# Interleaved rows, wider value tiles and earlier weights in a fused sliding-window attention and gated-unit kernel

## The chip, the cores and the metric

The kernel runs on one core of one Trainium2 chip. The metric is the device time of one execution in microseconds (us), the median of several. A core has a matrix engine (TensorE, PE in the profile; its weight loads are PEld), VectorE (DVE), ScalarE (ACT), GpSimd (POOL), SyncE (SP), and 16 DMA engines that move data between device memory (HBM) and the on-chip memory. Transfers are issued from the queues of SP, ACT and POOL.

## The reference

Eight batches, eight heads, 576 positions, head size 64, all float32. Heads 0 to 3 see the 32 positions up to their own ("plain"), heads 4 to 7 see every fourth of the last 128 ("dilated"). The attention output, 512 wide, goes into a gated unit: a causal depthwise convolution of five taps gives the gate, `w_val` the value, `w_out` the output.

```python
scores = scale * np.matmul(q, k.transpose(0, 1, 3, 2))
mask_plain = (rel >= 0) & (rel < window)                                   # window 32
mask_dil = (rel >= 0) & (rel < window * dilation) & (rel % dilation == 0)  # dilation 4
attn = softmax(where(mask, scores, -1e9)); x = (attn @ v) with heads side by side
gate_pre += conv_w[k][None, None, :] * xp[:, k:k + S, :]                   # for k in range(5)
gate = 1.0 / (1.0 + np.exp(-gate_pre)); val = x @ w_val
return (gate * val @ w_out)
```

## The kernel before

**Work.** The unit of attention is a pair of heads; there are 32 pairs, four to a batch, dilated and plain in turn (`order`, line 216). For each pair `attend` (L532) makes scores (`scores`, L460) into two PSUM banks, exponentials on ACT (L463), a multiplication by a 0/1 mask on DVE or POOL (L468), the product with v (L477 plain, L487 and L491 dilated), the division by the row sum on DVE (L496, L497), a transpose (L514, L518) and a copy into `xT` (L388 on ACT, L390 on DVE). When a batch has its four pairs, `gated` (L638) makes for each of four chunks the convolution (L591), a tanh (L648), the value product (L601) and gate times value (L652), and then the output product (L609), its copy to `osb` (L614, L616) and the store to HBM (L666). Each batch has 64 rows that don't fill a tile; `y_rem` (L659) collects them over four batches, and L673 stores them, twice in a kernel, two stores each.

**Loads of q and k.** Two batches, four heads of one kind, are a group, cut into three tiles of 128 partitions (`rows`, L311; `load_rows`, L328, issued at L331). Tile u = 0 is the first batch's first 128 partition rows, u = 2 the second batch's last 128, and the middle tile, u = 1, takes 64 rows of each batch. A partition row is 3072 bytes: one transfer of 384 KB for a dilated tile; for a plain middle tile two of 192 KB. There are 4 groups x 2 kinds = 8 middle tiles for q and 8 for k. A dilated tile is transposed as it stands (`transpose_in`, L377 to L384, by a product with the identity `ident`); a plain one is first cast on POOL into `qc` or `kc` (L414). The transposed tile goes to `qT` or `kT` on ACT or DVE.

**Loads of v.** A dilated pair has two tiles, `va` (partition rows 0 to 95) and `vz` (rows 64 to 143, so 80 rows), loaded at L362 and cast by POOL at L560 into `vda` and `vdb`. A plain pair has one tile `vp`, loaded by one transfer at L368 and two at L371, in pieces of 256 bytes.

**Weights.** `load_w` (L700) loads `w_val` and `w_out` by POOL's queue, three transfers each (L704, L705), casting on the way. `ldwv` is due after the load of the plain middle tile of q in group 0, `ldwo` after v of pair 4. Copies on ACT and DVE put `w_val` in order (L715), then two transfers of SP (L718, `swap_out`) make the second copy of `w_out`.

**Order.** `Plan.run` (L52) simulates the kernel at build time with the costs given to `add`, and emits every task in the order so found; the engines run their queues in that order. For a transfer it takes bytes and a rate (`lag`). In the built program the transfers of SP and ACT share eight semaphores in turn, and the issue of a transfer waits until the one before it on its semaphore has landed. So a store in ACT's queue can wait for a load that SP issued up to eight transfers ahead, and what is behind the store on ACT waits too.

Of the kernel before, what the change touches and what calls it, by code (L numbers as in the profile page):

```python
# [33 lines left out]
class Plan:  # L34
# [7 lines left out]
    SLACK = 0.1  # L42

# [8 lines left out]
    def run(self):  # L52
# [13 lines left out]
        while todo:  # L66
# [45 lines left out]
            if t.lag:  # L112
                free[e] = est + c
                nbytes, rate = t.lag
                if e == "SP":
# [22 lines left out]
def kernel(  # L138
# [48 lines left out]
    vas = bufs(NVD, [96, 2, R * D], FP32, "va")  # L187
    vzs = bufs(NVD, [80, 2, R * D], FP32, "vz")
    vd0 = bufs(NVD, [96, 2, R, DA], BF16, "vda")
    vd1 = bufs(NVD, [80, 2, R, DA], BF16, "vdb")  # L190
# [71 lines left out]
    def c_spread_p():  # L262
# [3 lines left out]
                              mask_p[:, None, 96:192].to_broadcast([128, 6, 96]))  # L266

# [33 lines left out]
    K_sp = add("sp", -5, {"DVE": 0.9}, lambda t: c_spread_p(), [K_mp])  # L301
    K_id2 = add("id2", 0.5, {"DVE": 0.4}, lambda t: c_ident2(), [K_ident])
# [8 lines left out]
    def rows(kind, u):  # L311
# [21 lines left out]
    def unit(n, kind):  # L333
        for u in range(3):
            first = 8 * n + (0, 2, 4)[u] + (kind == "p")
            for w, (nm, ring, src) in enumerate((("q", qs, q), ("k", ks, k))):
# [7 lines left out]
                    "ld" + nm, first + 0.1 * w, 393.0 / len(pieces), 330.0,  # L344
# [6 lines left out]
    def load_v(i):  # L351
# [25 lines left out]
    def transpose_in(t, kind, src):  # L377
        ps = bank(t, BF16)
        for f in range(6):
# [4 lines left out]
            nc.tensor.transpose(out=ps[:, f * 128:f * 128 + 128], in_=lhs, identity=ident)  # L384
# [17 lines left out]
    def prepare(n, kind, u):  # L402

        prio = 8 * n + (0, 2, 4)[u] + (kind == "p")
        for nm in "qk":
# [4 lines left out]
            if kind == "p":  # L410
# [9 lines left out]
            tr = U["tr"] = add("tr", prio - 0.05, {"PE": 0.34}, lambda t, src=src: transpose_in(t, kind, src),  # L420
                               got + [K_ident], banks=1, mode="full")
# [11 lines left out]
    def scores(t, i, hf, qT, kT):  # L433
# [3 lines left out]
        for x in range(2):  # L437
            rb = slice(x * D, x * D + D)
            if is_dil(i):
# [5 lines left out]
                for n in range(2):  # L445
                    g0 = ((b % 2) * 4 + 2 * (g - 2) + n) * 48
                    o = hf * 3 * G + 3 * g0 + 64
# [332 lines left out]
```

## Time and profile before

| what | value |
|---|---|
| median of 3 runs (lowest to highest) | 361.05 us (357.87 to 362.71) |
| profiled execution, its time | 360.51 us |
| profiled execution, its span | 358.80 us |
| PE busy, PEld busy | 208.7 us, 140.9 us |
| DVE, ACT, POOL busy | 129.2 us, 110.1 us, 57.5 us |
| moved by DMA | 42.33 MB, mean 118 GB/s |
| mean granted clock of TensorE | 0.793 |
| last PE instruction ends | 348.3 us |

The profile is of one execution. "PE busy" counts matmuls; PEld overlaps it. The page cuts the span into 40 slices of 8.97 us and gives each engine's busy share in tenths. "DMA" is the mean busy share of the 16 DMA engines. The chain is followed back from the last instruction, at each step to what released it. A line such as "ACT qTd L388 <- DMA k" names the idle engine, the instruction that then ran, and what released it; where one wait is for several things, the one that came last.

### The profile page before, as it was taken

To read this page: it belongs to the slowest core of one execution; us is meant where nothing else is said; L and a number is where in the kernel's file an instruction comes from. 1 tells how busy PE (TensorE), PEld (TensorE's weight loads), DVE (VectorE), ACT (ScalarE), POOL (GpSimd) and SP (SyncE) were. 2 spreads that over 40 slices of the span, in tenths; PEclk is the share of its full clock that TensorE was granted. 3 is DMA by queue.
4 is the path that set the end of the run, shared out by engine and by line. 5 is a ranking of instruction groups with operands and counts; after the bars stand their busy time and mean duration, and the time that the engine had idled before them with its cause. 6 is when DMAs were issued, how large, how long until landed. Compare 5 with 4: busy or idle time off the path is not lost.

```text
span 358.8 us, 5844 instructions
## 1 busy us (share of the span) xinstructions
PE 208.7 (58%) x2452; PEld 140.9 (39%) x2452; DVE 129.2 (36%) x221; ACT 110.1 (31%) x174; POOL 57.5 (16%) x98
## 2 busy tenths in 40 slices
PE   3317055755028766678616575756672787666970
PEld 2214044535024534545414453434432565444530
DVE  5313116643012435344600534441340366345240
ACT  3123035141032333430214244534023445413420
POOL 6203035060100041003500041030100031020000
PEclk9999999978556868655955989886576599766997
DMA  7225399921169146321277029222139421100331
GB/s 238 67 84 96 91 271 244 206 87 54 50 216 237 47 136 201 97 87 50 74 220 239 2 50 321 60 82 83 50 90 294 134 46 60 60 0 2 119 119 58
DMA packets 47490, 42.33 MB, mean 118 GB/s; under 512 B 26851, under 2 KB 39656, under 8 KB 47464
## 3 DMA queue, kind: packets, MB, share of 16 engines
q1 hardware_dynamic: 41424, 31.46, 31.9%
q10 hardware_dynamic: 4920, 9.45, 7.1%
q0 software_dynamic: 1120, 1.05, 2.0%
q8 instruction: 19, 0.31, 0.4%
q14 instruction: 7, 0.06, 0.1%
HBM read 33.04 MB, written 9.44 MB: 118 GB/s over the span
## 4 chain that ended last, share of the span: by engine, by line
PE 41%; DMA 14%; DVE 14%; ACT 11%; SPq 11%; issue 4%; POOL 1%; ACTq 1%; DVEq 0%; POOLq 0%
DMA k<-in_k_dram 11%; PE ps L601 11%; PE ps L609 10%; PE ps L591 7%; SPq L331 7%; ACT et L463 6%; DVE xn L497 5%; DVE y L652 5%; PE ps L384 5%; ACT gate L648 3%; SPq L371 3%; PE ps L460 3%; DVE rec L496 2%; PE ps L477 2%; DMA va<-in_v_dram 2%
## 5 line engine op out<-in xcount | busy, mean ns | idle before, releaser
L601 PE MATMUL ps<-xT,w_val 128*128 128x288 bf16 x256 | 48.9, 352 | 11.6 <-ACT et L463 4.8
L463 ACT ACTIVATE et<-ps 128x576 bf16<-128x576 f32 x64 | 39.9, 650 | 43.9 <-PE ps L460 14.4
L591 PE MATMUL ps<-xT,conv_d 64*64 64x288 bf16 x640 | 37.2, 377 | 20.3 <-ACT osb L614 12.6
L609 PE MATMUL ps<-w_out,y 128*128 128x512 bf16 x128 | 40.3, 455 | 7.2 <-DVE xn L497 4.1
L601 PEld LDWEIGHTS <-w_val 128*128 128x128 bf16 x256 | 29.1, 118 | 25.9 <-issue 11.8
L614 ACT ACTIVATE osb<-ps 128x512 f32<-128x512 f32 x33 | 19.5, 597 | 53.2 <-PE ps L609 27.9
L652 DVE SCALAR_TENSOR_TENSOR y<-gate,ps 128x576 bf16<-128x576 bf16 x32 | 23.6, 751 | 31.9 <-PE ps L601 14.3
L591 PEld LDWEIGHTS <-conv_d 64*64 64x64 bf16 x640 | 23.4, 136 | 27.3 <-issue 22.6
L496 DVE RECIPROCAL rec<-ps 96x8 f32<-96x8 f32 (+1 forms) x48 | 10.1, 210 | 62.6 <-ACT et L463 23.7
L648 ACT ACTIVATE gate<-ps 128x576 bf16<-128x576 f32 x32 | 20.3, 652 | 34.0 <-PE ps L591 9.6
L390 DVE COPY xT<-ps 128x576 bf16<-128x576 bf16 x15 | 11.4, 757 | 51.9 <-ACT gate L648 18.5
L460 PE MATMUL ps<-qTd,kTd 64*128 64x96 bf16 (+1 forms) x256 | 10.8, 223 | 29.4 <-ACT gate L648 22.3
L497 DVE TENSOR_TENSOR xn<-ps,rec 96x512 bf16<-96x512 f32 (+1 forms) x32 | 26.2, 820 | 1.1
L659 POOL COPY y_rem<-y 128x256 bf16<-128x256 bf16 x8 | 3.2, 399 | 139.0 <-DVE y L652 139.0
L388 ACT COPY xT<-ps 128x576 bf16<-128x576 bf16 x17 | 10.9, 639 | 41.2 <-DVE y L652 16.7
L609 PEld LDWEIGHTS <-y 128*128 128x128 bf16 x128 | 13.4, 112 | 24.0 <-issue 17.1
L460 PEld LDWEIGHTS <-kTd 64*128 64x128 bf16 x256 | 8.3, 111 | 34.1 <-issue 31.2
L468 DVE TENSOR_TENSOR et<-et,mask_d 128x1152 bf16<-128x1152 bf16 x15 | 12.4, 827 | 25.4 <-ACT et L463 25.4
L560 POOL CAST vda<-va 96x512 bf16<-96x512 f32 x16 | 10.6, 664 | 65.1 <-DMA va<-in_v_dram 32.1
L468 DVE TENSOR_TENSOR et<-et,mask_p 128x1152 bf16<-128x1152 bf16 x14 | 13.1, 938 | 13.9 <-ACT et L463 13.9
L460 PE MATMUL ps<-qTp,kTp 64*128 64x96 bf16 x192 | 9.3, 226 | 9.7 <-DVE y L652 3.9
L384 PE MATMUL ps<-ident,qc 128*128 128x128 bf16 x72 | 7.8, 261 | 11.4 <-POOL qc L414 5.0
(73 smaller groups left out, 256.4 us busy)
## 6 DMA issues: line engine op xcount, KB each, us to landing
out_dram<-osb ACTq DMA_DIRECT2D x16, 512.0 KB
q<-in_q_dram SPq DMA_DIRECT2D x20, 384.0 KB
k<-in_k_dram SPq DMA_DIRECT2D x20, 384.0 KB
vp<-in_v_dram SPq DMA_DIRECT2D x32, 160.0 KB
va<-in_v_dram SPq DMA_DIRECT2D x16, 192.0 KB
vz<-in_v_dram SPq DMA_DIRECT2D x16, 160.0 KB
q<-in_q_dram SPq DMA_DIRECT2D x8, 192.0 KB
k<-in_k_dram SPq DMA_DIRECT2D x8, 192.0 KB
```

The source lines that it names most:

```text
L331: nc.sync.dma_start(out=dst[:, o:o + w], in_=bass.AP(tensor=src.tensor, offset=base + off, ap=ap))
L384: nc.tensor.transpose(out=ps[:, f * 128:f * 128 + 128], in_=lhs, identity=ident)
L460: nc.tensor.matmul(out=o, lhsT=l, rhs=r, start=True, stop=True)
L463: nc.scalar.activation(out=et[:, hf * 576:hf * 576 + 576].rearrange("p (b c) -> p b c", b=2), in_=ps[:, :, 0:HALF], func=AF.Exp, scale=scale)
L468: eng.tensor_tensor(out=et[:, 0:ET], in0=et[:, 0:ET], in1=(mask_d if is_dil(i) else mask_p)[:, 0:ET], op=ALU.mult)
L497: nc.vector.tensor_tensor(out=xo, in0=av[:, :, :, 0:D], in1=rec[:, :, 0:n, None].to_broadcast([96, 2, n, D]), op=ALU.mult)
L591: nc.tensor.matmul(out=ps[ob:ob + D, half, 0:HALF], lhsT=conv_d[x * D:x * D + D, c, kk, :], rhs=xT[x * D:x * D + D, c, s:s + HALF], start= ...
L601: nc.tensor.matmul(out=ps[:, half, 0:HALF], lhsT=w_val[half][:, mc, c * 128:(c + 1) * 128], rhs=xT[:, mc, s:s + HALF], start=(mc == 0), st ...
L609: nc.tensor.matmul(out=ps[:, :], lhsT=cols(c), rhs=w_out[half][:, c, :], start=(c == 0), stop=(c == NCH - 1))
L614: nc.scalar.activation(out=osb, in_=ps, func=AF.Copy, scale=0.5)
L648: th = add("tanh", base + 1.0 + 0.5 * c, {"ACT": 0.66}, lambda t, cv=cv, gt=gt: nc.scalar.activation(out=gt, in_=banks(cv, 2)[:, :, 0:HALF ...
L652: y = add("y", base + 1.2 + 0.5 * c, {"DVE": 0.76}, lambda t, c=c, vl=vl, gt=gt: nc.vector.scalar_tensor_tensor(out=y_all[:, c, b % NY, :] ...
```

## The change

The core of the diff (each hunk is whole where the text speaks of it):

```diff
+    TRANSFER = 1.1
...
                 nbytes, rate = t.lag
+                rate /= self.TRANSFER
...
-    vas = bufs(NVD, [96, 2, R * D], FP32, "va")
-    vzs = bufs(NVD, [80, 2, R * D], FP32, "vz")
-    vd0 = bufs(NVD, [96, 2, R, DA], BF16, "vda")
-    vd1 = bufs(NVD, [80, 2, R, DA], BF16, "vdb")
+    vas = bufs(NVD, [128, 2, R * D], FP32, "va")
+    vzs = bufs(NVD, [128, 2, R * D], FP32, "vz")
+    vd0 = bufs(NVD, [128, 2, R, DA], BF16, "vda")
+    vd1 = bufs(NVD, [128, 2, R, DA], BF16, "vdb")
...
-    y_rem = consts.tile([128, NCH, 2, B, 32], BF16, name="y_rem")
+    y_rem = consts.tile([128, NCH, 2, 2, 32, 4], BF16, name="y_rem")
+    ident_x = consts.tile([128, 128], BF16, name="ident_x")
...
-        band(mask_d[:, 192:240].rearrange("p (m t) -> p m t", m=3), 32, [[1, 3], [3, 16]], 1)
+        band(mask_d[:, 192:240].rearrange("p (m t) -> p m t", m=3), 96 - (T - 128), [[1, 3], [3, 16]], 1)
...
+    def c_identx():
+        nc.vector.tensor_copy(ident_x.rearrange("p (b r) -> p b r", b=2), ident.rearrange("p (r b) -> p b r", b=2))
...
-            part, off = [[step, 2], [r * D, 64]], 128 * r * D
+            part, off = [[r * D, 64], [step, 2]], 128 * r * D
...
-                    "ld" + nm, first + 0.1 * w, 393.0 / len(pieces), 330.0,
+                    "ld" + nm, first + 0.1 * w, 393.0 / len(pieces), 390.0 if kind == "d" else 330.0,
...
-            for x, (dst, r0, n) in enumerate(((vas[j % NVD], 0, 96), (vzs[j % NVD], 64, 80))):
-                P["lv"].append(ld("ldv", i + 0.2 + 0.1 * x, n * 2.05, 240.0,
+            for x, (dst, r0, n) in enumerate(((vas[j % NVD], 0, 128), (vzs[j % NVD], T - 128, 128))):
+                P["lv"].append(ld("ldv", i + 0.2 + 0.1 * x, n * 2.05, 380.0,
...
-            nc.tensor.transpose(out=ps[:, f * 128:f * 128 + 128], in_=lhs, identity=ident)
+            nc.tensor.transpose(out=ps[:, f * 128:f * 128 + 128], in_=lhs, identity=ident_x if u == 1 else ident)
...
-                    nc.tensor.matmul(out=ps[:, x, c * DA:(c + 1) * DA], lhsT=et[0:96, o:o + 128],
+                    nc.tensor.matmul(out=ps[:, x, c * DA:(c + 1) * DA], lhsT=et[:, o:o + 128],
...
-                    nc.tensor.matmul(out=ps[:, x, c * DA:(c + 1) * DA], lhsT=et[0:80, o:o + 128],
+                    nc.tensor.matmul(out=ps[:, x, c * DA:(c + 1) * DA], lhsT=et[:, o:o + 128],
...
-                    out=out[b - 3:b + 1, half * HALF + 256:half * HALF + HALF, :], in_=osb[:, half, :]), 262.0)
+                    out=out[b - 3:b + 1, half * HALF + 256:half * HALF + HALF, :].rearrange("b n d -> n b d"),
+                    in_=osb[:, half, :]), 262.0)
...
     wv = add("ldwv", 1.0, {"POOL": 2.6}, lambda t: load_w(t, w_out[1], moe_w_val),
-             [UNIT[0, "p", 1, "q"]["ld"][0]], lag=(1049.0, 330.0))
+             [PAIR[1]["lv"][0]], lag=(1049.0, 330.0))
...
     wo = add("ldwo", 5.0, {"POOL": 2.6}, lambda t: load_w(t, w_out[0], moe_w_out),
-             [PAIR[4]["lv"][0]], lag=(1049.0, 330.0))
+             [PAIR[3]["lv"][0]], lag=(1049.0, 330.0))
```

In words. The middle tile's partitions take rows of the two batches in turn (row 0 of the first, row 0 of the second, row 1 of the first), where before the first 64 were one batch and the last 64 the other. The transpose of a middle tile uses `ident_x`, the identity with its columns permuted, which puts the rows back in the old order; all transposes now wait for its making. `va` and `vz` have 128 partitions (rows 0 to 127, and 16 to 143), and the dilated products with v contract over 128 partitions. The mask of the second part is moved to fit. `y_rem` holds the four batches of a row side by side, and its stores walk row by row with the batch inside. `ldwv` is due after the first piece of v of pair 1, `ldwo` after v of pair 3. The planner's rates are changed (also that of stores, from 340 to 400), and all are divided by 1.1, so that it orders some tasks differently. In the built program PE, DVE, ACT and POOL have nearly the same lists as before: POOL's mask multiplications go from 3 to 2 (DVE's from 29 to 30), ACT's copies of `w_val` from 2 to 4 (DVE's from 6 to 4). POOL issues `ldwv` ahead of the two casts of pair 2's v where it was behind them, and `ldwo` ahead of the first cast of pair 4's v. In SP's queue the two `swap_out` transfers come seven loads earlier, ahead of the first tile of group 1.

More of the change, by code (lines that the diff above doesn't have):

```diff
@@ L301 @@
     K_sp = add("sp", -5, {"DVE": 0.9}, lambda t: c_spread_p(), [K_mp])
+    K_idx = add("idx", 0.4, {"DVE": 0.2}, lambda t: c_identx(), [K_ident])
     K_id2 = add("id2", 0.5, {"DVE": 0.4}, lambda t: c_ident2(), [K_ident])
@@ L374, in load_v, with transpose_in @@
                                 ap=[[D, 128], [96 * D, NB - 1], [1, D]])), dep))
-    def transpose_in(t, kind, src):
+    def transpose_in(t, kind, src, u):
         ps = bank(t, BF16)
@@ L419, in prepare @@
                 src = c
-            tr = U["tr"] = add("tr", prio - 0.05, {"PE": 0.34}, lambda t, src=src: transpose_in(t, kind, src),
-                               got + [K_ident], banks=1, mode="full")
+            tr = U["tr"] = add("tr", prio - 0.05, {"PE": 0.34}, lambda t, src=src: transpose_in(t, kind, src, u),
+                               got + [K_idx], banks=1, mode="full")
             if kind == "d":
@@ L446, in scores @@
                     g0 = ((b % 2) * 4 + 2 * (g - 2) + n) * 48
-                    o = hf * 3 * G + 3 * g0 + 64
+                    o = hf * 3 * G + 3 * g0 + T - 128
                     todo[x].append((ps[:, x, 192 + n * 48:240 + n * 48], kT[rb, o:o + 128],
@@ L558, in attend @@
             c0, c1 = vd0[j % NVD], vd1[j % NVD]
-            for x, (s, d, n) in enumerate(((vas[j % NVD], c0, 96), (vzs[j % NVD], c1, 80))):
+            for x, (s, d) in enumerate(((vas[j % NVD], c0), (vzs[j % NVD], c1))):
                 P[f"cv{x}"] = add("cv", i - 0.2, {"POOL": 0.62}, lambda t, s=s, d=d: nc.gpsimd.tensor_copy(
@@ L634, in out_tiles @@
             ots.append(ot)
-        out_st.append([add("st", prio + 0.5, {"ACT": 0.40}, lambda t, e=e: e(osb), oes, lag=(nb, 340.0)) for e, nb in store])
+        out_st.append([add("st", prio + 0.5, {"ACT": 0.40}, lambda t, e=e: e(osb), oes, lag=(nb, 400.0)) for e, nb in store])
         return ots
@@ L659, in gated @@
         YB[b] = add("yrem", base + 3.0, {"POOL": 0.35}, lambda t: nc.gpsimd.tensor_copy(
-            y_rem[:, :, :, b, :], yv[:, :, :, 256:HALF]), ys)
+            y_rem[:, :, :, b // 4, :, b % 4], yv[:, :, :, 256:HALF]), ys)
         YO[b] = [YB[b]]
@@ L670, in gated @@
             out_tiles(base + 5.2, [
-                (half, lambda c, half=half: y_rem[:, c, half, b - 3:b + 1, :].rearrange("p b n -> p (b n)"), deps)
+                (half, lambda c, half=half: y_rem[:, c, half, b // 4, :, :].rearrange("p n b -> p (n b)"), deps)
                 for half in range(2)],
                 [(lambda osb, half=half: nc.scalar.dma_start(
-                    out=out[b - 3:b + 1, half * HALF + 256:half * HALF + HALF, :], in_=osb[:, half, :]), 262.0)
+                    out=out[b - 3:b + 1, half * HALF + 256:half * HALF + HALF, :].rearrange("b n d -> n b d"),
+                    in_=osb[:, half, :]), 262.0)
                  for half in range(2)])
```

## Prediction

> **What bounds the kernel now.** I read the page's 40 slices first, then stretches, then the queues of ACT and SP around the longest idle time of PE.
>
> ```profile
> PE   3317055755028766678616575756672787666970
> PEclk9999999978556868655955989886576599766997
> DMA  7225399921169146321277029222139421100331
> GB/s 238 67 84 96 91 271 244 206 87 54 50 216 237 47 136 201 97 87 50 74 220 239 2 50 321 60 82 83 50 90 294 134 46 60 60 0 2 119 119 58
> PE 41%; DMA 14%; DVE 14%; ACT 11%; SPq 11%; issue 4%; POOL 1%; ACTq 1%; DVEq 0%; POOLq 0%
> ```
>
> No engine is full. PE has holes near 15, 24, 42, 95, 183 and 272 us, and each follows slices at 50 to 100 GB/s. A quarter of the chain is DMA and SP's queue. In the stretches below the columns are length, busy time of PE, PEld, DVE, ACT and POOL (instructions), PE's granted clock, DMA share, GB/s. The first two show a plateau, the next two the DMA at work on other loads.
>
> ```profile
> 20.00:26.00 6.00, 0.00 (x0) 0.00 (x0) 0.76 (x1) 0.48 (x1) 0.00 (x0) 1.00 0.13 51
> 84.00:99.00 15.00, 2.06 (x51) 1.70 (x49) 2.03 (x3) 0.00 (x0) 2.00 (x3) 0.72 0.13 50
> 2.00:10.00 8.00, 2.98 (x33) 2.28 (x34) 4.38 (x9) 3.45 (x5) 5.08 (x20) 1.00 0.91 273
> 48.00:60.00 12.00, 7.05 (x105) 5.37 (x103) 6.22 (x6) 6.74 (x10) 6.91 (x9) 1.00 1.19 243
> ```
>
> 0.13 is 2 of 16: two DMA engines work, 14 stand, while middle tiles load (outermost count 2 in HBM). Tiles with 128 outermost run at 273 GB/s. The queues show how PE gets stuck:
>
> ```profile
> 86.61 7.28 SPq L331 DMA_DIRECT2D k<-in_k_dram  x2
> ```
> ```profile
> 102.06 0.45 ACTq L666 DMA_DIRECT2D out_dram<-osb  x1
> 102.61 0.80 ACT L388 COPY qTd<-ps 128x768 bf16<-128x768 bf16 x1 [19.36 <-DMA k<-in_k_dram]
> ```
>
> SP issues the plain middle tile of k at 86.6; the last byte comes at 102. A store in ACT's queue waits for it by the shared semaphore, and with it everything on ACT behind the store: 19.36 us idle. PE then has nothing to do. The holes:
>
> ```profile
> 12.30:17.10 4.80, 0.02 (x1) 0.02 (x2) 0.69 (x1) 0.80 (x1) 0.00 (x0) 1.00 0.26 77
> 19.20:26.40 7.20, 0.05 (x1) 0.00 (x0) 0.76 (x1) 1.19 (x2) 0.00 (x0) 1.00 0.16 55
> 35.60:47.30 11.70, 0.82 (x6) 0.56 (x7) 1.45 (x3) 0.65 (x1) 1.65 (x2) 1.00 0.45 122
> 87.10:104.60 17.50, 0.04 (x2) 0.04 (x3) 0.06 (x1) 1.90 (x3) 2.00 (x3) 0.60 0.28 92
> 177.20:189.10 11.90, 1.41 (x20) 1.04 (x20) 0.43 (x1) 1.74 (x3) 0.00 (x0) 0.59 0.72 213
> 268.50:276.90 8.40, 1.42 (x20) 0.98 (x20) 0.00 (x0) 1.75 (x4) 0.83 (x1) 0.69 0.91 270
> ```
>
> Length less PE's busy time: 4.8 + 7.2 + 10.9 = 22.9 us at the start, 17.5 at 95, and 10.5 + 7.0 in the last two, 57.9 us in all.
>
> **The change part by part**, against the profiled execution's 360.5 us (span 358.8 and 1.7 around it; the median of the runs is 0.5 above).
>
> *Middle tiles interleaved.* The outermost count in HBM becomes 64. Counts of 128, 4 and 2 in this trace went at 16, 4 and 2 engines (273, 102 and 50 GB/s; the 102 is below), so I take 16. The same bytes in rows of the same length: a 384 KB tile takes 393/50 = 7.9 us now and 393/273 = 1.4 us then. The holes go: -57.9. What is late next?
> - Start. The last load that PE waits for is the second piece of the plain middle tile of k, SP's 17th transfer. Up to it there are 8 tiles of q and k (3.15 MB), two dilated v (1.05 MB, new size), one plain v (0.39 MB) and the first weights (1.05 MB): 5.6 MB at 273 GB/s is 20.6 us, and with 3 us for the first transfer (issued at 0.8, used at 4.0) 23.6 us. PE came there at 39.8, less the 15.4 us of holes before: 24.4. So it just fits. Bounds 0 and 5 (the rate 225 instead of 273, below the 243 of the row with 256-byte pieces); I take 2, near the fit.
> - Pair 8. PE came to it at 104.6, less 22.9 and 17.5: 64 us. It needs all of group 0 (4.72 MB), v of pairs 0 to 8 (4.2), weights (2.1), the swap (0.5), its own first tile (0.8): 12.3 MB, at 243 GB/s 51 us, and 3. It fits by 10. SP is also blocked while the swap waits for the copies of `w_val`, which now stands ahead of the seven loads that pair 8 and its followers need; in the old trace the swap was issued at 62.4 after a wait of 1.7. Bounds 0 and 8, I take 3.
> - Stores in ACT's queue still wait for the load on their semaphore. Eight transfers ahead at 1.0 to 1.4 us each, most landed already: 0 to 6 over the three places, I take 2.
>
> *v over 128 partitions.* It adds (32 + 48) x 2 KB x 16 = 2.6 MB, some 10 us of DMA at 273 GB/s over the kernel, hidden: the share of the DMA is 0.43 at most in the stretches between the holes. What precedes the 17th transfer is counted above. POOL's casts (614 ns for 96 as for 80 partitions), the products and the weight loads have the same free sizes: 0, and not more than 32 casts x 0.05 = 1.6 us on POOL, which has 57.5 busy of 358.8.
>
> *Identity.* One copy on DVE of 128 x 128; its nearest row, a 128 x 512 copy to `w_val`, took 0.28 us. It is covered by the first load, used at 4.0. Cost 0, and 0.3 if that cover were gone.
>
> *Weights earlier.* Three issues on POOL (0.69 + 0.69 + 0.73 = 2.1 us) come ahead of the two casts of pair 2's v. Those end 2.1 us later; who waits is the product with v of pair 2, behind scores, two exponentials and a mask. 0 to 2.1; I take 1. The transfers' bytes are in the sums above. The software queue took 2.0% of 16 engines, 7.2 us for both weights. The Trainium skill ("DMA: Bandwidth & Descriptors", section "Issuing engines are not separate DMA queues") speaks against this edit: transfers of all queues share the same 16 engines and interleave, so weights put ahead of the start's loads delay them; by that rule alone 3.6 us, half of the 7.2, would be added, and the sum would be 307.
>
> *Remainder stores.* The last two stores are the end of the chain:
>
> ```profile
> GB/s 0 0 0 0 0 0 0 370 353 0 0 331 370 45 0 0 0 0 0 0 0 0 141 384 198 379 345 34 11 56 76 102 102 102 102 102 37 0 0 11
> 348.39 1.21 ACTq L673 DMA_DIRECT2D out_dram<-osb  x2
> ```
>
> The slices are 0.725 us from 330 on. Two stores of 262 KB take 5.1 us at 102 GB/s; at the 370 of the stores before them 1.4. The row count 32 comes outermost instead of the batch count 4: -3.7, bounds -4.5 (latency shared) and 0.
>
> *Clock.* Half clock follows some holes:
>
> ```profile
> 104.60:114.60 10.00, 8.64 (x69) 4.80 (x69) 2.67 (x4) 2.78 (x5) 0.00 (x0) 0.50 0.92 251
> 148.70:169.00 20.30, 16.52 (x162) 11.54 (x162) 8.86 (x14) 6.25 (x10) 2.36 (x1) 0.50 0.23 73
> 333.00:345.00 12.00, 10.86 (x111) 6.67 (x109) 4.78 (x7) 3.82 (x7) 0.40 (x1) 1.00 0.24 89
> ```
>
> With the hole at 95 gone, the 10 us behind it may run at full clock and save up to half of 8.6. But 148.7 to 169 shows half clock with PE 81% busy and no hole before it. Bounds -15 (half of the PE time in two such stretches and the parts after the later holes) and +10 (one more stretch like the middle one); I take -4, the stretch right behind the hole. The Trainium skill ("TensorE: Matmul & The Clock Gate", section "HAM oscillation") holds that gaps over about 3.4 us throttle the array to half; the first row agrees, the second does not. By the rule alone no hole would mean full clock: PE's 41% of the chain, 147 us at 0.793, would be 117, and the sum 277.
>
> Sum: 360.5 - 57.9 + 2 + 3 + 2 + 1 - 3.7 - 4 = 302.9, so **303 us**. Cross-check: pair 8 to 16 took 87.9 us and 16 to 24 took 84.5 (by the exponentials at 105.0, 192.9, 277.4); less their holes, 77.4 each; from 277.4 to the end 81.4, less 3.7. With pair 8 at 64 that gives 64 + 3 x 77.5 + 1.7 = 298.
>
> **Rivals.**
> - *B, half of the holes come back.* The loads are spread, but the order of SP's and ACT's queues, and the 256-byte pieces of v, keep PE waiting. For: in 48 to 60 the DMA share is above 1 and PE only 59% busy. Against: that stretch makes up for two plateaus. Half of 57.9 is 29, in place of my allowances of 7: 303 + 22 = 325.
> - *C, the clock gains more.* All stretches as 333 to 345. Down to the bound: 303 - 11 = 292, and with nothing late, 284.
> - *D, the loads stay on two engines*, because the split goes by something other than the outermost count. Then only the stores gain: 360.5 - 3.7 = 357. Against: the counts 128, 4 and 2 above.
> - *E, slower.* One mechanism: PE's clock. Where PE never rests, half clock is granted throughout, as in 148.7 to 169. 147 us of PE on the chain would be 147 x 0.793/0.5 = 233: 303 + 86 = 389. It decides from a mean clock of 0.57 down (147 x (0.793/0.57 - 1) = 57). Against: 333 to 345, busiest of all, at 1.00.
>
> **How the numbers follow.** The forecast 0.71 (its own range 288 to 318), B 0.15, C 0.08, D 0.03, E 0.03. Low end: 360.5 - 57.9 - 3.7 - 15 = 284. High end: no clock gain and all upper bounds, 298.9 + 5 + 8 + 6 + 2 = 320, and on past B's 325 to 328. That leaves out half of B, some of C, D and E, under 2 in 10. Faster by over 2% (about what a measurement of this kernel can tell from no change): 0.71 + 0.15 + 0.08 = 0.94; within 2%: D, 0.03; slower: E, 0.03.
>
> **What would show it.** Right: no stretch at 0.13 DMA share and 50 GB/s; ACT's wait of 19.36 us gone, PE's first hole over 3 us near 12 us short or absent; pair 8's exponentials at 62 to 70 us; the last two stores in under 2 us. Wrong: middle tiles still at 50 GB/s (D); holes as long behind ACT's stores or SP's swap (B); a mean clock under 0.6 (E).

## The result and the profile after

The changed kernel takes 276.23 us (median, 275.91 to 276.66) beside 361.88 us for the kernel before on the same chip: 0.766 of its time, 95% interval [0.760, 0.773]. The forecast was 303 (284 to 328): the direction was right, and the gain of 85.6 us was under-estimated by 27. The profiled execution took 275.91 us, its span 274.2, and the mean granted clock is 0.842 where it was 0.793. The ratios here and below leave out runs over 1.5% above the fastest of their kernel, while the medians hold every run.

The slices of the changed kernel, 6.86 us each, and the shares of its chain:

```profile
PE   3766598688764677875766557778666686968772
PEclk9997779999977757997779975589999956865999
DMA  7999999991895505880039791095401410000306
GB/s 244 335 280 312 254 299 323 329 334 31 267 305 156 207 2 122 252 278 2 0 66 325 195 306 70 20 327 162 148 2 48 122 43 2 0 2 13 143 2 229
PE 52%; DVE 19%; ACT 13%; DMA 7%; issue 4%; SPq 3%; ACTq 0%; DVEq 0%
```

The runs of slices at 50 to 100 GB/s are gone, and so are the empty digits of PE between its second slice and its last. DMA and SP's queue go from 25% of the chain to 10%, PE from 41% to 52%. In the stretches, each from the first exponential of pair 8, 16 and 24 to the next, the columns are length, busy time of PE, PEld, DVE, ACT and POOL (instructions), granted clock, DMA share and GB/s. Before:

```profile
0.00:105.00 105.00, 42.61 (x563) 31.50 (x564) 33.97 (x66) 27.21 (x42) 26.64 (x54) 0.90 0.55 138
105.00:192.90 87.90, 57.50 (x628) 38.10 (x627) 31.85 (x53) 25.80 (x42) 12.37 (x17) 0.67 0.49 146
192.90:277.40 84.50, 53.65 (x610) 34.47 (x606) 29.91 (x48) 28.53 (x45) 11.06 (x17) 0.76 0.37 112
277.40:358.80 81.40, 54.95 (x670) 36.84 (x664) 33.46 (x55) 28.59 (x47) 7.39 (x10) 0.81 0.21 69
```

After, with the busiest stretch of the start as a fifth line:

```profile
0.00:56.50 56.50, 37.90 (x588) 28.81 (x592) 31.66 (x66) 28.33 (x47) 22.53 (x50) 0.91 1.06 299
56.50:120.00 63.50, 44.52 (x620) 31.60 (x613) 29.52 (x49) 26.58 (x44) 14.41 (x19) 0.84 0.63 192
120.00:193.00 73.00, 50.75 (x598) 33.15 (x598) 28.42 (x47) 29.06 (x46) 14.89 (x19) 0.79 0.49 150
193.00:274.20 81.20, 57.08 (x656) 37.35 (x653) 34.27 (x55) 29.38 (x47) 5.98 (x9) 0.85 0.18 61
4.00:13.00 9.00, 6.41 (x78) 5.33 (x78) 6.36 (x12) 3.02 (x6) 7.04 (x11) 1.00 1.10 344
```

The work of the first stretch takes 56.5 us instead of 105: its transfers run at 299 GB/s, and the best 9 us at 344, where the forecast had 273. The second stretch saves 24.4 us though it held no hole that the forecast had listed but the one at 183 (10.5), the third 11.5 (it held 7.0), the last 0.2, its shorter stores included. Of the 24.4 us, 13.0 are PE's busy time (57.50 to 44.52), at a granted clock of 0.84 where it was 0.67. So the gain goes past the holes, and the question is whose it is.

At the start, SP issues the two pieces of the plain middle tile of k from 11.19 us on; the chain has the first landed at 17.64 (11.19 + 6.45), and POOL's cast of the tile, which needs both, starts at 18.72:

```profile
11.19 1.25 SPq L338 DMA_DIRECT2D k<-in_k_dram  x2
```
```profile
11.19 6.45 DMA k<-in_k_dram
```
```profile
18.72 1.22 POOL L421 CAST kc<-k 128x768 bf16<-128x768 f32 x1 [1.20 <-DMA k<-in_k_dram]
```

The forecast had the second piece in at 23.6. ACT's wait of 19.36 us is gone; the longest that is left on ACT is 7.9 us, for PE. PE's only idle time over 2.5 us is the 4.1 us before its first load. The last two stores are over sooner (slices of 0.605 us from 250 us on):

```profile
269.31 1.24 ACTq L680 DMA_DIRECT2D out_dram<-osb  x2
```
```profile
GB/s 0 0 0 0 0 142 389 335 0 0 0 250 383 234 27 0 0 0 0 0 0 0 0 0 0 0 0 0 132 386 349 186 389 315 372 383 88 0 0 14
```

The 372, 383 and 88 near the end are the two stores, 0.51 MB in 1.4 us; the old ones crept up over 11, 56 and 76 to 102 GB/s and took nine slices of 0.725, 6.5 us.

### The profile page after: what moved, and what is told of

Read it like the earlier page. It is cut to its first block, busy times and chain, and to the rows that moved or that the text cites. A ratio compares the mean times of both kernels' runs of the same rounds, so it can differ in the third digit from the quotient of the medians.

```text
span 274.2 us, 5860 instructions
## 1 busy us (share of the span) xinstructions
PE 190.2 (69%) x2452; PEld 130.9 (48%) x2452; DVE 123.9 (45%) x217; ACT 113.3 (41%) x180; POOL 57.8 (21%) x97
## 4 chain that ended last, share of the span: by engine, by line
PE 52%; DVE 19%; ACT 13%; DMA 7%; issue 4%; SPq 3%; ACTq 0%; DVEq 0%
PE ps L608 15%; PE ps L616 11%; PE ps L598 9%; ACT et L470 7%; DVE xn L504 7%; DVE y L659 6%; DMA k<-in_k_dram 5%; PE ps L391 4%; PE ps L467 4%; ACT gate L655 3%; DVE rec L503 3%; DVE xm L504 3%; PE ps L521 2%; PE ps L484 2%; PE ps L525 1%
## 5 line engine op out<-in xcount | busy, mean ns | idle before, releaser
L608 PE MATMUL ps<-xT,w_val 128*128 128x288 bf16 x256 | 46.7, 343 | 7.4 <-DVE xm L504 2.4
L616 PE MATMUL ps<-w_out,y 128*128 128x512 bf16 x128 | 34.5, 410 | 7.6 <-DVE xn L504 4.2
L598 PE MATMUL ps<-xT,conv_d 64*64 64x288 bf16 x640 | 31.9, 331 | 11.0 <-ACT et L470 5.1
L659 DVE SCALAR_TENSOR_TENSOR y<-gate,ps 128x576 bf16<-128x576 bf16 x32 | 23.6, 752 | 31.7 <-PE ps L608 20.9
L666 POOL COPY y_rem<-y 128x256 bf16<-128x256 bf16 x8 | 6.1, 757 | 121.7 <-DVE y L659 121.7
L395 ACT COPY xT<-ps 128x576 bf16<-128x576 bf16 x21 | 13.4, 639 | 40.3 <-PE ps L525 20.9
L621 ACT ACTIVATE osb<-ps 128x512 f32<-128x512 f32 x30 | 17.5, 598 | 27.7 <-PE ps L616 20.4
L598 PEld LDWEIGHTS <-conv_d 64*64 64x64 bf16 x640 | 21.4, 121 | 15.5 <-issue 10.8
L475 DVE TENSOR_TENSOR et<-et,mask_d 128x1152 bf16<-128x1152 bf16 x16 | 12.0, 754 | 17.2 <-ACT et L470 17.2
L467 PE MATMUL ps<-qTd,kTd 64*128 64x96 bf16 (+1 forms) x256 | 10.1, 207 | 11.5 <-DVE xn L504 4.0
L475 DVE TENSOR_TENSOR et<-et,mask_p 128x1152 bf16<-128x1152 bf16 x14 | 11.5, 822 | 10.0 <-ACT et L470 10.0
L475 POOL TENSOR_TENSOR et<-et,mask_p 128x1152 bf16<-128x1152 bf16 x2 | 4.7, 2360 | 52.0 <-ACT et L470 52.0
L567 POOL CAST vda<-va 128x512 bf16<-128x512 f32 x16 | 10.1, 628 | 25.1 <-issue 18.6
L397 DVE COPY xT<-ps 128x576 bf16<-128x576 bf16 x11 | 8.3, 756 | 12.1 <-PE ps L525 5.5
```

The costliest lines, as they stand in the source:

```text
L395: nc.scalar.copy(out=out_, in_=in_)
L467: nc.tensor.matmul(out=o, lhsT=l, rhs=r, start=True, stop=True)
L475: eng.tensor_tensor(out=et[:, 0:ET], in0=et[:, 0:ET], in1=(mask_d if is_dil(i) else mask_p)[:, 0:ET], op=ALU.mult)
L598: nc.tensor.matmul(out=ps[ob:ob + D, half, 0:HALF], lhsT=conv_d[x * D:x * D + D, c, kk, :], rhs=xT[x * D:x * D + D, c, s:s + HALF], start= ...
L608: nc.tensor.matmul(out=ps[:, half, 0:HALF], lhsT=w_val[half][:, mc, c * 128:(c + 1) * 128], rhs=xT[:, mc, s:s + HALF], start=(mc == 0), st ...
L616: nc.tensor.matmul(out=ps[:, :], lhsT=cols(c), rhs=w_out[half][:, c, :], start=(c == 0), stop=(c == NCH - 1))
```

## The experiments

Each time is a median; the ratio is to the kernel before, run beside it, with its 95% interval. "PE", "idle" and "tail" split the profiled span: PE's busy time, its idle time up to its last instruction, and what follows that.

| kernel | us | ratio | span | PE | idle | tail | clock |
|---|---|---|---|---|---|---|---|
| before | 361.88 | | 358.8 | 208.7 | 139.6 | 10.5 | 0.793 |
| after | 276.23 | 0.766 [0.760, 0.773] | 274.2 | 190.2 | 79.0 | 5.0 | 0.842 |
| a1 | 293.06 | 0.807 [0.792, 0.823] | 290.6 | 190.9 | 88.9 | 10.7 | 0.820 |
| a2 | 352.53 | 0.980 [0.971, 0.988] | 352.6 | 200.5 | 147.1 | 5.0 | 0.790 |
| a3 | 276.46 | 0.758 [0.749, 0.768] | 272.0 | 185.0 | 81.9 | 5.1 | 0.890 |
| b0 | 300.57 | 0.834 [0.827, 0.841] | 298.9 | 192.1 | 101.8 | 5.0 | 0.861 |
| b1 | 304.03 | 0.842 [0.833, 0.851] | 303.6 | 193.5 | 105.1 | 5.0 | 0.812 |
| b2 | 277.1 | 0.761 [0.750, 0.773] | 271.5 | 179.9 | 86.6 | 5.0 | 0.935 |
| b3 | 290.84 | 0.805 [0.796, 0.813] | 289.4 | 194.3 | 90.1 | 5.0 | 0.813 |
| b4 | 281.98 | 0.782 [0.776, 0.788] | 280.4 | 190.6 | 79.3 | 10.5 | 0.830 |

The clock column counts the time ahead of a trace's first clock record as 1.00 (63 us in before, 52 in b0, 49 in b2, 14 in after; see the last section), so its rows can't be compared closely; "PE" can.

The first theory after the result was that the interleaved loads are the whole mechanism and the sizes of the other terms were wrong; its rivals were that the planner's new order, or the clock, gave the rest.

### a1: the interleave alone

The kernel before with the interleaved rows and `ident_x`, and nothing else.

```diff
-            part, off = [[step, 2], [r * D, 64]], 128 * r * D
+            part, off = [[r * D, 64], [step, 2]], 128 * r * D
...
-            nc.tensor.transpose(out=ps[:, f * 128:f * 128 + 128], in_=lhs, identity=ident)
+            nc.tensor.transpose(out=ps[:, f * 128:f * 128 + 128], in_=lhs, identity=ident_x if u == 1 else ident)
```

> The kernel before with one part of the change: interleaved rows in the middle q/k tiles, with the permuted identity. Theory 1 (the loads on two engines are the whole of it, and what was mis-sized is PE's clock and the small gaps that went with the holes): 280 to 286 us, that is the changed kernel's 276 plus 3.7 for the last stores and a few for the start; no stretch at 0.13 DMA share; PE busy near 190 us. Theory 2 (what the prediction missed, some 27 us, came from the other parts: the planner's new order, the wider v, the earlier weights): 295 to 303 us, near the 303 forecast, and PE busy near 200 or more.

Measured: 293.06 us, some 69 less than before. The time lies between the ranges of the two theories, and PE's busy time is that of theory 1.

```profile
PE 190.9 (66%) x2440; PEld 132.0 (45%) x2452; DVE 128.5 (44%) x222; ACT 110.0 (38%) x174; POOL 56.7 (20%) x98
```

PE's idle time falls by 50.7 us, as the forecast had it (57.9 of holes less allowances of 7). But PE's busy time falls as well, from 208.7 to 190.9 for the same matmuls, and the forecast had 4 for that. (The trace lacks the records of 12 output products, which hides up to 1.8 us of busy time.) The stretches of a1, cut at the same exponentials, show where:

```profile
0.00:68.10 68.10, 42.67 (x563) 31.76 (x565) 32.47 (x67) 27.23 (x43) 26.08 (x54) 0.77 0.95 242
68.10:136.90 68.80, 47.35 (x622) 33.03 (x624) 31.79 (x53) 25.95 (x42) 12.29 (x17) 0.83 0.54 158
136.90:211.50 74.60, 49.27 (x606) 32.14 (x603) 30.82 (x48) 28.36 (x46) 10.93 (x17) 0.82 0.46 137
211.50:290.60 79.10, 51.63 (x661) 35.02 (x662) 33.45 (x55) 28.46 (x47) 7.38 (x10) 0.86 0.18 61
```

Up to pair 8 PE is as busy as before (42.67 and 42.61 us), and its idle time falls by 37.0: the 40.4 us of holes less 3.4. Behind pair 8 PE's busy time falls by 10.2, 4.4 and 3.3 us.

### a2: all but the interleave

The changed kernel with the rows and the identity of before.

```diff
-            part, off = [[r * D, 64], [step, 2]], 128 * r * D
+            part, off = [[step, 2], [r * D, 64]], 128 * r * D
...
-            nc.tensor.transpose(out=ps[:, f * 128:f * 128 + 128], in_=lhs, identity=ident_x if u == 1 else ident)
+            nc.tensor.transpose(out=ps[:, f * 128:f * 128 + 128], in_=lhs, identity=ident)
```

> The changed kernel with the middle tiles' rows and identity as before, all else changed. Theory 1: 352 to 360 us, the time before less 3.7 for the stores; holes as in the kernel before. Theory 2: 330 to 340 us, since the order, the wider v and the weights would give over 20 us by themselves.

Measured: 352.53 us, 0.980 of before, in the range of theory 1. All the rest is worth some 7 to 9 us while the plateaus stay, and its idle time, 147.1, is even above that of before. What it gives behind spread loads is 16.8 (a1 less after).

### b0 and b1: the holes put back, one group at a time

The changed kernel with the middle tiles of group 0 (b0) or of group 1 (b1) on two DMA engines; this is b1, and b0 has `n == 0`.

```diff
-            part, off = [[r * D, 64], [step, 2]], 128 * r * D
+            part, off = [[r * D, 64], [step, 2]][::-1 if n == 1 else 1], 128 * r * D
...
-            nc.tensor.transpose(out=ps[:, f * 128:f * 128 + 128], in_=lhs, identity=ident_x if u == 1 else ident)
+            nc.tensor.transpose(out=ps[:, f * 128:f * 128 + 128], in_=lhs, identity=ident_x if u == 1 and n != 1 else ident)
```

> The changed kernel, where only the first group's middle tiles are on two engines again; same order. Theory 1: the start's holes come back, about 23 us, and PE stays at half clock through the start (six transposes at about 0.80 us and not 0.35), so PE's busy time grows by 3 to 6 us: 301 to 308. Rival (holes alone): 297 to 301, PE busy within 2 us.

> The changed kernel, where only the second group's four middle tiles (of q and k, dilated and plain) are put on two engines again; the order is the same. It prices one hole. Theory 1 (a hole costs its length and the clock around it): PE's idle time grows by 10 to 17 us and PE's busy time by 4 to 8 us, 292 to 300 us. Rival (a hole costs its length alone, the clock has other causes): idle time grows by the same, PE busy by less than 2 us, 286 to 292.

Measured: +24.3 us for group 0, +27.8 for group 1. In b1 the holes stand in two stretches:

```profile
56.80:64.60 7.80, 0.00 (x0) 0.00 (x1) 0.96 (x1) 1.13 (x3) 0.00 (x0) 0.71 0.21 80
67.60:83.30 15.70, 0.01 (x2) 0.00 (x0) 0.00 (x0) 0.66 (x2) 0.00 (x0) 0.50 0.41 128
```

They are 23.5 us almost without a matmul. How PE gets stuck shows on ACT:

```profile
82.11 0.48 ACTq L673 DMA_DIRECT2D out_dram<-osb  x1
82.64 1.19 ACT L655 ACTIVATE gate<-ps 128x576 bf16<-128x576 f32 x2 [17.02 <-DMA vp<-in_v_dram]
```

A store in ACT's queue waits for a load that SP issued late, and a gate behind the store waits with it, 17.02 us: the mechanism that the forecast read from before. PE's idle time grows by 26.1 in b1 and 22.8 in b0, its busy time by 3.3 and 1.9. So a hole costs its length, and PE's slower work around it 2 to 3 us for a group (the traces of b0 and b1 lack 13 records each, worth some 0.6 us). By its time and busy time b0 fits the rival, holes alone; b1 lies above both ranges, for its idle time grew by more than the 10 to 17 us expected.

### f4 and e1: what makes the load use 16 engines

f4 loads each middle tile by two transfers of 64 partitions, with the plain identity and every queue in the order of after; e1 makes the two halves separate tasks, for which the planner finds another order.

```diff
+        if u == 1:
+            (rd, _), (step, _), inner = ap
+            for x in range(2):
+                nc.sync.dma_start(out=dst[64 * x:64 * x + 64, o:o + w],
+                                  in_=bass.AP(tensor=src.tensor, offset=base + off + x * step, ap=[[rd, 64], inner]))
+            return
```

> The changed kernel without interleaved rows and without the permuted identity: each middle tile is loaded by two transfers, one for each batch's 64 partitions, with 64 outermost. If the number of engines follows the outermost count: no stretch at 0.13 DMA share, 275 to 281 us (eight tiles' transfers more for SP to issue, some 0.45 us each). Rival (something else about the middle tiles, such as two distant pieces of memory, is slow): 300 us or more.

> The changed kernel with each middle tile's transfer cut into two of 64 partitions (64 outermost), no interleaving, plain identity, and every queue in the changed kernel's order. If the outermost count sets the number of engines and the 299 us of the other version came from its order: 275 to 279 us. Rival (the two halves load slowly in themselves): 290 us or more, with a DMA share near 0.13 or 0.5 while they load.

Measured: e1 299.18 us (0.820 [0.811, 0.829]), f4 281.56 (0.766 [0.760, 0.773]; the time of before beside it was higher too). In f4 the start runs at:

```profile
4.00:13.00 9.00, 4.42 (x55) 3.73 (x56) 3.94 (x8) 2.17 (x4) 4.32 (x9) 1.00 1.04 269
```

A share of 1.04 is all 16 engines, so it is the outermost count (64) and not the interleaving that sets how many work. The Trainium skill ("DMA: Bandwidth & Descriptors", section "Why a DMA increments its semaphore by 16 and not by 1") says that a transfer takes the largest number up to 16 that divides the slowest dimensions of both its sides. The rows here agree: 2 gave a share of 0.13, 4 gave 102 GB/s, 64 gave a share of 1.04. By the two medians the interleave is some 5 us better than two halves, though by the ratios they can't be told apart. e1 is 18 us slower than f4 with 64 outermost in both. Its order is another one, and it loads each half of a plain tile by one transfer where f4 has two; which of these costs the 18 us is not separated.

### a3 and b2: wide v and the planner's rates

a3 is the changed kernel with v over 96 and 80 partitions as before, b2 with the planner's rates of before.

```diff
-            for x, (dst, r0, n) in enumerate(((vas[j % NVD], 0, 128), (vzs[j % NVD], T - 128, 128))):
+            for x, (dst, r0, n) in enumerate(((vas[j % NVD], 0, 96), (vzs[j % NVD], 64, 80))):
...
-                    nc.tensor.matmul(out=ps[:, x, c * DA:(c + 1) * DA], lhsT=et[:, o:o + 128],
+                    nc.tensor.matmul(out=ps[:, x, c * DA:(c + 1) * DA], lhsT=et[0:96, o:o + 128],
```
```diff
-    TRANSFER = 1.1
+    TRANSFER = 1.0
...
-                P["lv"].append(ld("ldv", i + 0.2 + 0.1 * x, n * 2.05, 380.0,
+                P["lv"].append(ld("ldv", i + 0.2 + 0.1 * x, n * 2.05, 240.0,
```

> The changed kernel with v of dilated pairs over 96 and 80 partitions as before (with the planner's new rate, so that its order shifts a little). Theories O and W: 274 to 280 us; the wider v is worth nothing and costs 2.6 MB. Theory V (128 partitions load better): 281 to 288.

> The changed kernel with the planner's old rates (no division by 1.1; 330 for q and k, 240 for dilated v, 340 for stores). Only the order of the queues differs. Interleaving alone came to 293, the changed kernel to 276, so 17 us are in the other parts. Theory O (the order made with truer rates gives most of what the stores don't): 284 to 290 us, with more idle time of PE in the first two batches. Theory W (the earlier weights give it): 275 to 279.

Measured: 276.46 and 277.1 us; neither is to be told from after, so the rates do not give what theory O expected of them. The 2.6 MB that the wide v adds are hidden, as forecast.

### b4: the remainder stores as before

The changed kernel with the batch outermost in `y_rem` and its stores.

```diff
-                    out=out[b - 3:b + 1, half * HALF + 256:half * HALF + HALF, :].rearrange("b n d -> n b d"),
+                    out=out[b - 3:b + 1, half * HALF + 256:half * HALF + HALF, :].rearrange("b n d -> b n d"),
```

> The changed kernel with the remainder rows stored as before, batch outermost; the order of all queues is the same. All theories: 279.5 to 282 us. The prediction's -3.7 gives 279.9; the traces' times from PE's last instruction to the end (10.5 and 5.0) give 281.7.

Measured: 281.98 us, +5.75; the tail is 10.5 us and not 5.0, and PE's busy and idle times are those of after. The part is worth 5.75 and not 3.7: the forecast took the plateau of 102 GB/s for the whole transfer and left out the ramp before it.

### b3, d1 and d2: weights earlier, or another order

b3 is the changed kernel with the due times of the weights of before.

```diff
-             [PAIR[1]["lv"][0]], lag=(1049.0, 330.0))
+             [UNIT[0, "p", 1, "q"]["ld"][0]], lag=(1049.0, 330.0))
...
-             [PAIR[3]["lv"][0]], lag=(1049.0, 330.0))
+             [PAIR[4]["lv"][0]], lag=(1049.0, 330.0))
```

> The changed kernel with the weights due as before (after the plain middle tile of q, and after v of pair 4). Theory W: 283 to 289 us, the first value products and the swap later. Theory O: 275 to 279.

Measured: 290.84 us, 14.6 above after and just above the range of theory W, where by the forecast's price (a cost of 1) it would be 1 below. Either the weights come in time only with the change, or the planner makes a better order with the new due times. d1 keeps the order of after and moves only POOL's issue of the weights back; d2 keeps the order of b3 and moves it ahead.

```diff
+    emitted = plan.run()
+    for load, cast in ((wv, PAIR[2]["cv1"]), (wo, PAIR[4]["cv0"])):
+        emitted.remove(load)
+        emitted.insert(emitted.index(cast) + 1, load)
```

> The changed kernel with every queue in its own order, but POOL's: the value weights' load stands behind the two casts of pair 2's v and the output weights' load behind the first cast of pair 4's, as when they are due as before. With due times as before (and the order that the planner makes of them) the time was 291, 15 us more than the changed kernel's 276. Theory A (the weights arrive late, and the value products wait): 284 to 291 us, the first value product after 36 us. Theory P (the arrival matters little; the order that the planner makes of it costs the 15 us, POOL's casts stuck behind the gather of the remainder rows above all): 275 to 279 us.

> The reverse: the order that the planner makes with the weights due as before (291 us), but POOL issues the two loads as early as in the changed kernel. Theory A: 275 to 281 us. Theory P: 288 to 292 us; POOL's second cast of pair 6's v still behind the gather of the remainder rows, by 15 us or so.

Measured: d1 277.1 us (0.765 [0.757, 0.774]), d2 291.73 (0.805 [0.797, 0.813]). Both lie in the ranges of theory P: the time follows the order. When the weights come does not matter to within what the runs can tell. POOL issues the value weights at 16.1 us in d1 where it did at 10.4 in after, and the value products begin at 37.0 us (the first row) where they did at 33.7, but the time is the same within 0.9. In d2 they begin at 38.0 (the second row), and the time is 14.6 above that of d1.

```profile
L608 PE MATMUL ps<-xT,w_val x256: 282/286/448, 37.0 to 263.5; 128*128 128x288 bf16 x128
```
```profile
L608 PE MATMUL ps<-xT,w_val x256: 282/286/448, 38.0 to 277.6; 128*128 128x288 bf16 x128
```

Where does the order cost it? The stretch from 40 to 60 us, first of d1, then of d2:

```profile
40.00:60.00 20.00, 16.23 (x261) 11.45 (x262) 12.09 (x21) 9.24 (x16) 3.29 (x5) 0.96 0.98 308
```
```profile
40.00:60.00 20.00, 12.66 (x139) 8.11 (x137) 7.79 (x13) 5.41 (x9) 6.76 (x8) 0.80 0.73 193
```

PE does 261 matmuls in the one and 139 in the other. PE's queue in d2 (start, length, operation, and in brackets the idle time before it and what ended it):

```profile
48.77 0.30 PE L467 MATMUL ps<-qTp,kTp 64*128 64x96 bf16 x6 [0.80 <-DVE y L659]
49.79 0.41 PE L467 MATMUL ps<-qTp,kTp 64*128 64x96 bf16 x11 [0.72 <-ACT et L470]
50.92 1.08 PE L598 MATMUL ps<-xT,conv_d 64*64 64x288 bf16 x20 [0.72 <-ACT et L470]
...
52.79 0.38 PE L494 MATMUL ps<-vda,et 128*128 128x65 bf16 x4 [0.45 <-ACT et L470]
...
53.96 0.38 PE L498 MATMUL ps<-vdb,et 128*128 128x65 bf16 x4 [0.58 <-ACT et L470]
54.92 0.49 PE L484 MATMUL ps<-vp,et 128*128 128x65 bf16 x6 [0.58 <-DVE xn L504]
```

And the same work in d1:

```profile
47.78 0.82 PE L467 MATMUL ps<-qTp,kTp 64*128 64x96 bf16 x18 [0.74 <-ACT gate L655]
48.54 0.42 PE L494 MATMUL ps<-vda,et 128*128 128x65 bf16 x8
48.87 0.42 PE L498 MATMUL ps<-vdb,et 128*128 128x65 bf16 x8
49.41 1.89 PE L616 MATMUL ps<-w_out,y 128*128 128x512 bf16 x8
51.13 0.54 PE L484 MATMUL ps<-vp,et 128*128 128x65 bf16 x12
```

In the rows of d2 the small pieces of PE's work wait 0.45 to 0.8 us for a step of ACT or DVE, one after the other, with little independent work between. In d1 it waits once and then runs five groups without a gap. The first exponential of pair 8 comes at 60.2 us in d1 and at 66.5 in d2, that of pair 16 at 124.0 and 138.4, and that of pair 24 at 194.9 and 204.9. So 6.3 us of the loss have arisen by pair 8, 8 more arise between pairs 8 and 16, and the rest moves back and forth by some 4 us. This is read from the traces; no run mends one stretch alone. POOL's cast of a v does stand behind the gather of the remainder rows in d2, which waits 14.20 us for its rows (until 48.78), as theory P had it; what that costs is not shown.

### f2, f1, g2, g1 and f3: which step of the order

Suspects in the old order were the copies of `w_val` and the masks that POOL makes (2.36 us for one, where DVE takes 0.75 to 0.82). f2 is d2 with the copies put behind the copy into `xT` of pair 2, which makes them 10 us earlier (25.6 for 35.9); g1 and g2 keep the orders of after and of b3 and do POOL's masks on DVE at their place; f3 and f1 forbid POOL the masks in after and in b3 and let the planner make the order anew.

```diff
+    for x in K_wv:
+        emitted.remove(x)
+    at = emitted.index(PAIR[2]["evx"]) + 1
+    emitted[at:at] = K_wv
```
```diff
+        if t.name == "mk":
+            t.engine = "DVE"
```
```diff
-        mk = P["mk"] = add("mk", i, {"DVE": 0.84, "POOL": 2.4}, lambda t: masks(t, i, et),
+        mk = P["mk"] = add("mk", i, {"DVE": 0.84}, lambda t: masks(t, i, et),
```

The first diff is f2's, the second that of g1 and g2, the third that of f3 and f1.

> The slow order (291 us) with the weights issued early and the eight copies of w_val moved on ACT and DVE to behind the third pair, where the changed kernel has them; PE's and SP's order unchanged. Theory C (the copies, right ahead of the first value product, hold the chain): 283 to 288 us, the first batch's value products 2 to 4 us sooner and the rest kept. Theories M and Q: 288 to 292 us.

> The kernel with weights due as before (291 us), with all masks on DVE (0.75 us each, where POOL takes 2.36 for each of its three). Theory M (a mask on POOL, behind which POOL's casts and PE's products wait, makes the slow order slow): 276 to 282 us. Theory Q (the order of PE's work in the first two batches does): 287 to 293 us.

> The changed kernel with all masks on DVE; the planner makes a new order. Theory M: 272 to 276 us, 1.6 us less on each of the two masks that POOL had. Theory Q: anything from 272 to 290, by the order that comes out.

> The changed kernel, every queue in its own order, its two POOL masks (2.36 us each) done by DVE (0.75 us each). Theory M (the masks on POOL themselves cost the time): 262 to 270 us, of the 16 that the version with no masks on POOL gains. Theory Q (the planner's new order does it): 273 to 276.5, at most 1.6 us for each of the two masks.

> The version with the weights due as before (291 us), every queue in its order, its three POOL masks done by DVE. Theory M: 279 to 284 us. Theory Q: 286 to 292.

| kernel | order | us | ratio |
|---|---|---|---|
| f2 | of b3, copies moved | 293.92 | 0.803 [0.794, 0.813] |
| g2 | of b3, masks on DVE in place | 293.46 | 0.816 [0.808, 0.825] |
| g1 | of after, masks on DVE in place | 273.2 | 0.763 [0.755, 0.770] |
| f1 | new, due times of b3 | 280.75 | 0.769 [0.763, 0.775] |
| f3 | new, due times of after | 260.26 | 0.711 [0.704, 0.718] |

By its time alone f1 falls in the range of theory M, and f3 below the ranges of both theories; g1 and g2, which move the masks and keep the order, come out as theory Q has it (g2 1.5 us above its range). Neither the copies (f2) nor the masks themselves (g2 no gain, g1 3 us by its median and none by its ratio) are what the old order pays for. But one cost taken from the planner changes the order, and with it the time by 10 and 16 us (f1 beside b3, f3 beside after). f3 beats both kernels of this case: 260.26 us. Which step of the order is to blame is not settled; that it is the order is.

### c1: a warm start

The changed kernel with 24 idle transposes of the identity while PE waits for its first load. They are work whose result is thrown away.

```diff
+        while warm[0]:
+            warm[0] -= 1
+            nc.tensor.transpose(out=ps[:, 0:128], in_=ident, identity=ident)
```

> The changed kernel with 24 transposes of the identity ahead of the first real one, in the 4 us in which PE waits for the first load; they add work and change no result. In the changed kernel six transposes took about 0.80 us at the start, as at half clock. If idle time sets the clock: full clock from about 5 us on instead of 14, 272 to 275 us. Rival (the chain of the first pairs is held by DMA, POOL, ACT and DVE, and PE's clock there costs nothing): 275.5 to 277.5, with the granted clock higher.

Measured: 276.05 us (0.765 [0.759, 0.771]), no change. But the edit did not warm PE. The first loaded tile is transposed no faster behind the idle transposes:

```profile
1.44 2.74 PE L390 MATMUL ps<-ident 128*128 128x128 bf16 x24 [1.44 <-POOL ident L236]
4.02 0.82 PE L396 MATMUL ps<-ident,q 128*128 128x128 bf16 x6
```

Six transposes still take 0.82 us at 17.2 us, where after had them in 0.51 at 15.3. The page's mean clock of 0.867 for 0.842 is no sign of warmth either: 19.5 us ahead of the first clock record count as 1.00 there, 13.6 in after, and the other three executions of c1 have 0.824 to 0.842. So the run does not say what a warm start would be worth.

## Why the prediction was right and wrong

**Right: the mechanism.** The forecast named the two working DMA engines, the store that waits in ACT's queue and the holes that follow. a1 shows the interleave to be worth some 69 of the 86 us. Its idle time fell by 50.7, where the forecast's holes less its three allowances are 50.9, and the parts agree too: 37.0 up to pair 8, where the holes less the 5 us for the start and pair 8 are 35.4. b0 and b1 put holes back and get their length back. Of the signs named, all but one came: no plateau, no long wait on ACT, the stores in 1.4 us. Pair 8's exponentials came at 56.5 and not at 62 to 70; in a1, with the old order and weights, they came at 68.1, so this sign was missed for the other parts of the change and not for the interleave.

**Right: costs of nothing.** Wide v (a3) and the rates (b2) are not to be told from zero; the identity's copy was priced by no run of its own, but PE's first transpose comes at 4.13 us where it came at 3.98.

**Wrong: the step "*Weights earlier* ... 0 to 2.1; I take 1".** It cost the edit by what POOL does late, and bounded it at zero from below. It is worth -14.6 (b3). Neither bound had a case for a planner that orders all tasks anew when one due time moves. The text of the change itself said that lists on the engines move; the forecast costed the moved DMA issues and took the rest for unchanged. Even POOL's 2.1 us, for which it charged 1, were hidden: in after the three issues end at 12.53 us, and the casts of pair 2's v then still wait 1.10 us for their load, until 13.63. The rule cited there, that transfers of all queues share the engines and so early weights delay the start's loads, was given a sum of 307 by an estimate: d1 and after, which differ in when the weights are issued, lie 0.9 us apart, within what the runs can tell, and with the sign against that delay.

**Wrong in size: "*Clock.* ... I take -4".** PE's busy time fell by 17.8 in a1 and 18.5 in after, beyond the lower bound of -15. In a1 that is 13.8 more than the 4 taken, and a1 beat the sum of its own terms (360.5 - 57.9 + 7 - 4 = 305.6) by 12.5. All of the fall lies behind pair 8. That the granted clock made PE's busy time fall is read from the traces. Split by the clock records, with the time ahead of the first one taken as half clock (last section), PE was busy for 87.3 us at full and 121.5 at half clock before, 108.3 and 82.6 in a1, 113.9 and 76.4 in after. The first plus half of the second is 148.0, 149.6 and 152.1: nearly the same work at another clock. Two things stay open. One is why so much more full clock was granted: b0 and b1 price it around a group's holes at 1.9 and 3.3 us, 5.2 of the 17.8. The other is how much of it the span keeps: b2's profiled execution has 10.3 us less of PE's busy time than that of after and is 2.7 us shorter (273.23 and 275.91), for PE's idle time is 7.6 us longer. The rule of the Trainium skill ("TensorE: Matmul & The Clock Gate", section "HAM oscillation") made 277 of it, near the result but not for its reason: the mean clock with no hole left (PE's longest idle time behind its first load is 2.4 us) is 0.842, not full, and the second hole of b1 does stand at 0.50.

**Wrong in size: "*Remainder stores* ... -3.7, bounds -4.5".** Measured -5.75 (b4). The line that the prediction quotes shows it: 11, 56 and 76 GB/s stand before the plateau. Nine slices of 0.725 us, less the 1.4 of now, would have given -5.1.

**The sum.** 12.5 for the interleave, 15.6 for the weights and 2.0 for the stores are 30.1 us beyond the forecast; the parts overlap by 3.5 (14.6 and 5.75 singly, 16.8 together from a1 to after), which leaves the 26.7 that were missed. The runs of a1 lie between 289.39 and 294.58, so these shares are good to 2 or 3 us.

**The rivals.** B (half of the holes come back) did not happen: the longest idle time of PE is 4.1 us, at the start. C, 284 to 292 by the clock, was nearest in number, but about half of what lay beyond the forecast was the order (15.6 of the 30.1). D and E are refuted: a share of 1.10 in the start's busiest stretch, and a mean clock that rose.

## What to carry to other kernels

Look at the outermost count of each slow transfer first: where a DMA share stands at 2 of 16, putting 64 outermost was worth nearly the full length of the holes behind it, and a store in a shared semaphore ring tells how the hole reaches the compute engines. Where a planner makes the order, no edit to a cost or due time is local: compare the new order with the old one on every engine, and give the edit a two-sided bound from what other orders of the same work cost (here 260 to 294 us). Read a transfer's ramp with its plateau.

## What the runs showed of the hardware

**The clock that the page shows before its first record is no measurement.** The page gives 1.00 for the first 63 us of before. But its six transposes ran there as slowly (0.82 us) as later at a recorded 0.50 (0.80; the clock's row for 104.6 to 114.6 is in the prediction), and at a recorded 1.00, between the two, they took 0.49:

```profile
47.30 0.82 PE L384 MATMUL ps<-ident,kc 128*128 128x128 bf16 x6 [7.46 <-POOL kc L414]
67.50 0.49 PE L384 MATMUL ps<-ident,qc 128*128 128x128 bf16 x6 [1.01 <-DVE xm L497]
105.72 0.80 PE L384 MATMUL ps<-ident,qc 128*128 128x128 bf16 x6 [0.50 <-ACT et L463]
```

In after, whose first record comes at 13.6 us, the same six took 0.50 us at a granted 1.00:

```profile
40.90 0.50 PE L391 MATMUL ps<-ident,kc 128*128 128x128 bf16 x6
```

So the first stretch of before ran at half clock too, which the forecast read as full. What that is worth on the path isn't known: c1's 24 transposes were meant to show it and did not speed up the first six (0.82 us).

**Busy time is no price.** In the profiled executions of after, a3 and b2 PE's busy time is 190.2, 185.0 and 179.9 us, and the times are 275.91, 273.71 and 273.23: of 10.3 us less busy time, 2.7 reach the end.
